# Decode attention beside a gated FFN on one core: head 0 of K loaded in two halves and taken out of VectorE's loop, the three large buffers at multiples of 4096 bytes

## The chip, the core and the metric

The kernel runs on one core of one Trainium2 chip. A core has TensorE (PE in the profile, PEld for its weight loads), VectorE (DVE), ScalarE (ACT), GpSimd (POOL) and SyncE (SP), which each run their own list of instructions and wait for one another through semaphores, and 16 DMA engines that move data between the main memory and the on-chip buffers (SBUF). The metric is the device time of one execution in microseconds, lower is better; times given are medians of several executions.

## What is computed

One token of a decoder layer in fp32. The input row x (576 values) is normalized; an attention block with 32 heads of 128 and a cache of 16384 positions, and a gated FFN of width 4608, both take the normalized row, and both results are added to x:

```
xn = _layernorm(x)
q = (xn @ wq).reshape(B, Sq, H, Dh).transpose(0, 2, 1, 3)
scores = einsum("bhqd,bhkd->bhqk", q, k_cache) * (Dh ** -0.5)
p = softmax(scores)
o = einsum("bhqk,bhkd->bhqd", p, v_cache)
out = x + o.transpose(0, 2, 1, 3).reshape(B, Sq, H * Dh) @ wo \
        + (gelu(xn @ w_gate) * (xn @ w_up)) @ w_down
```

K and V are 32 x 16384 x 128 fp32 each, 8.39 MB a head and cache, 537 MB of the 588 MB that the kernel reads. Each byte is used once.

## The kernel before

**Buffers.** Three large buffers, `slot_a`, `slot_b` and `slot_v` (`sa`, `sb`, `sv` in the code), hold 64 KB in each of the 128 partitions: one head of one cache, partition p holding 128 consecutive positions. They lie one behind the other in SBUF from byte 27904 of a partition on (`SLOT_AT`, L36; the allocation is at L124). Smaller tensors lie below. The weights pass through the same three buffers, before the attention and after it.

**Order.** Nothing is scheduled by a planner: each engine's list is written by hand. Outside the loops the class `Order` (L40) keeps a log of who wrote or read which columns, and puts the waits that follow from it ahead of an operation (`o.op`, behind `dve`, `act`, `pe_op`) or a DMA (`o.dma`, behind `load`). Inside the loops the semaphores are explicit: `take(e, s, n)` (L332) waits for `s` to reach n and takes n off.

**SP's queue.** All large loads are issued by SP, in this order: the q, gate and up weights; K of head 0 into `sb` and of head 1 into `sa` (L349 to L351, `load_k` counting on the semaphores `s_k[0]` and `s_k[1]`); V of head 0 into `sv`; then a loop of 15 passes, two heads each (L354): wait until DVE has released the K buffer (`s_kf`), load K of head h+2, wait until PE has released the V buffer (`s_vf`), load V of head h+1. After the loop come the first 28 row blocks of w_down into `sb`, V of head 31, the other w_down rows and the pieces of wo.

**One head.** ACT copies the head's q, spread over the partitions by PE, into `qs` (L398; `s_qd` tells DVE). DVE multiplies the K buffer in place by `qs` (L382, 128 x 16384), tells ACT through `s_qf` that `qs` may be overwritten, reduces each 128 products to a score in `S` (L384, result 128 x 128; two halves of `S` for even and odd heads), releases the K buffer (`s_kf`), takes each partition's largest score (L387) and, after a transposition by PE, the largest of all, negated (L389). ACT computes the exponentials `pe` and their sum (L402). PE multiplies them with V in 32 steps (L372) into `po` and releases the V buffer. A loop of 16 passes on DVE (L376) handles heads 0 and 1, 2 and 3, and so on, with `sb` for even and `sa` for odd heads.

**Before and after.** Ahead of head 0, DVE finishes the hidden row `hT` of the FFN (L322). Behind the loop it adds up the first 28 blocks of w_down, scaled by `hT` (L414 to L417), and PE projects the attention's result with wo; the last pieces of wo go into columns of `sb` that are already used up.

Of the kernel before, what the change touches and what calls it, by code (L numbers as in the profile page):

```python
# [10 lines left out]
ALU = mybir.AluOpType  # L11
AX = mybir.AxisListType

P = 128
H, SK, DH = 32, 16384, 128
D, DF = 576, 4608
R = SK // P
SUB = 64
# [14 lines left out]
WO_A = 20  # L33
WO_Q = 8
QUART = D // 4
SLOT_AT = 27904  # L36
SLOT_B = R * DH * 4


# [78 lines left out]
@with_exitstack  # L118
def kernel(ctx: ExitStack, tc: tile.TileContext, x, k_cache, v_cache, wq, wo, wg, wu, wd, out):
    nc = tc.nc  # L120
    ends = tc.alloc_semaphore("ends")
    slots = []
    for i, name in enumerate(("slot_a", "slot_b", "slot_v")):
        t = nc.alloc_sbuf_tensor_at(name, [P, R * DH], F32, offset=SLOT_AT + i * SLOT_B)  # L124
        SIZES[t.name] = R * DH
        slots.append(t.ap())
    i = nc.sync.dma_start(slots[0], wq[:DM].rearrange("(p j) f -> p (j f)", j=DJ)).then_inc(ends, 64)
    tc.no_tile_sem_insts.add(i.ins.name)
    tc.add_to_no_dep_group("first", i.ins)
    tc.declare_fence(nc.sync.nop().ins, group="first")  # L130
    with tc.tile_critical(sync_engine=mybir.EngineType.SP):
        decode(tc, x, k_cache, v_cache, wq, wo, wg, wu, wd, out, slots, ends)
    tc.no_sync_barrier()
    nc.sync.wait_ge(ends, 64)
# [19 lines left out]
def decode(tc, x, k_cache, v_cache, wq, wo, wg, wu, wd, out, slots, s_ends):  # L154
    nc = tc.nc
    o = Order(tc)
# [3 lines left out]
    def sem():  # L160
        return tc.alloc_semaphore(f"d{next(names)}")

    def sbuf(name, *shape):
        n = 1
        for s in shape[1:]:
            n *= s
        t = nc.alloc_sbuf_tensor(name, [P, n], F32)
        SIZES[t.name] = n
        return t.ap()[: shape[0]]

    def psum(name, banks):
        t = nc.alloc_psum_tensor(name, [P, 512 * banks], F32)
        SIZES[t.name] = 512 * banks
        return t.ap()

    kv, vv = (c.rearrange("b h (p n) d -> p (b h) (n d)", p=P) for c in (k_cache, v_cache))
# [7 lines left out]
    sa, sb, sv = slots  # L184
# [5 lines left out]
    qcur, qs = sbuf("qcur", 1, DH), sbuf("qs", P, DH)  # L190
    S = sbuf("scores", P, 2 * R)
# [3 lines left out]
    pm, nm, nb = sbuf("pm", P, 1), sbuf("nm", P, 1), sbuf("nb", P, 1)  # L195
    small = sbuf("small", P, 32)
    oT = sbuf("oT", P, WO_T)
    assert nc.sbuf_base <= SLOT_AT, nc.sbuf_base

# [3 lines left out]
    pt, pb, pc = pg[:, 512:1024], pg[:, 1024:], psum("pc", 1)  # L203
# [5 lines left out]
    def dve(name, out, *ins, **kw):  # L209
        o.op("vector", lambda e: getattr(e, name)(out, *ins, **kw), out, *[a for a in ins if isinstance(a, bass.AP)],  # L210
             *[a for a in kw.values() if isinstance(a, bass.AP)])
# [5 lines left out]
    def load(dst, src, **kw):  # L217
        o.dma(dst, src, sem(), **kw)
        return dst
# [13 lines left out]
    for i in range(2):  # L233
# [6 lines left out]
    s_q, s_m, s_n, s_o, s_e, s_v, s_po, s_pq, s_pt, s_pb, s_pc, s_vf, s_kf, s_qf, s_qd, s_d, s_a = (  # L240
        tc.alloc_semaphore(f"h{n}") for n in range(17))
    s_k = [tc.alloc_semaphore(f"k{n}") for n in range(2)]
# [45 lines left out]
    def q_part(h):  # L288
        r, lo = 32 * (h // (H // 4)), h % (H // 4) * DH
        return qb[r : r + 1, lo : lo + DH]  # L290
# [41 lines left out]
    def take(e, s, n=1):  # L332
        e.wait_ge(s, n).then_inc(s, -n)  # L333

    def head(h):
        return bass.ds(h, 1)
# [6 lines left out]
    def load_k(h, dst, s):  # L343
        nc.sync.dma_start(dst, kv[:, head(h), :].rearrange("p h f -> p (h f)")).then_inc(s_k[s], 16)
# [1 line left out]
    def load_v(h):  # L346
        nc.sync.dma_start(sv, vv[:, head(h), :].rearrange("p h f -> p (h f)")).then_inc(s_v, 16)

    for h, dst in ((0, sb), (1, sa)):  # L349
        o.wait("sync", [], [dst])  # L350
        load_k(h, dst, h)  # L351
    o.wait("sync", [], [sv])
    load_v(0)
    with nc.sync.Fori(0, (H - 2) // 2) as i:  # L354
# [18 lines left out]
               for k in range(32)], s_po)  # L373
        nc.tensor.drain().then_inc(s_vf, 1)

    with nc.vector.Fori(0, H // 2):  # L376
        for s, kt in ((0, sb), (1, sa)):
            blk = kt.rearrange("p (n d) -> p n d", d=DH)
            sc = S[:, s * R : s * R + R]
            take(nc.vector, s_k[s], 16)  # L380
            take(nc.vector, s_qd)
            nc.vector.tensor_mul(blk, blk, qs.unsqueeze(1).to_broadcast([P, R, DH])).then_inc(s_d, 1)  # L382
            nc.vector.wait_ge(s_d, 1).then_inc(s_qf, 1)
            nc.vector.tensor_reduce(sc, blk, axis=AX.X, op=ALU.add).then_inc(s_d, 1)  # L384
            nc.vector.wait_ge(s_d, 2).then_inc(s_kf, 1)
            take(nc.vector, s_d, 2)
            nc.vector.reduce_max(pm, sc, axis=AX.X).then_inc(s_m, 1)  # L387
            take(nc.vector, s_pt)
            nc.vector.tensor_reduce(nm[:1], pt[:1, :P], axis=AX.X, op=ALU.max, negate=True).then_inc(s_n, 1)  # L389

    for h0, n in ((0, 6), (6, 8), (14, 8), (22, 8), (30, 2)):
        row, lo = divmod(min(h0 + 2, H - 1), H // 4)
        with nc.scalar.Fori(0, n) as i:
# [11 lines left out]
            src = q_part(min(h0 + 2, H - 1)) if n == 2 else qb[32 * row : 32 * row + 1, bass.ds(i * DH + lo * DH, DH)]  # L405
# [102 lines left out]
```

## Time and profile before

| what | value |
|---|---|
| median of three runs | 1366.23 us (1365.65 to 1366.27) |
| the profiled execution, its own time | 1364.84 us |
| its span, first to last instruction | 1363.0 us |
| DVE busy | 1158.4 us |
| PE busy | 446.3 us |
| read from main memory | 587.60 MB |
| loads of K and V | 64 of 8.39 MB |

A line of the timeline has the start, the duration, the engine, the source line, the operation with its output and input, how many were merged, and in brackets how long the engine had been idle before it and what released it. Several instructions of one kind in a row are merged into one line that begins with the first. "DVEq" or "PEq" as releaser is a semaphore wait of the engine's own sequencer, whatever set the semaphore. A page's rows in 40 slices stand for 34.1 us each. A K buffer that has landed shows in DVE's multiplication, where DVE had been waiting; a V buffer in the first of PE's matmuls into `po`.

### The profile page before, as it was taken

How to read it: one execution, taken by the hardware profiler on the slowest of the kernel's cores; microseconds unless marked ns; L12 is line 12 of the kernel's file. 1: busy time of each engine (PE TensorE's matmuls, PEld its weight loads, DVE VectorE, ACT ScalarE, POOL GpSimd, SP SyncE). 2: the span in 40 equal slices, each digit the busy share in tenths (PEclk: the TensorE clock that was granted, in tenths of full speed). 3: DMA queues.
4: the chain of work that ended last, by engine and by line, in shares of the span. 5: the costliest groups of instructions: out<-in, count | busy, mean ns of one | idle time of the engine just before them, and what ended most of it. 6: DMA issues, size and time to landing. Idle time of an engine off the chain costs nothing. (4 is left out here: it accounts for less than half of the span.)

```text
span 1363.0 us, 7778 instructions
## 1 busy us (share of the span) xinstructions
PE 446.3 (33%) x3012; PEld 161.7 (12%) x3012; DVE 1158.4 (85%) x193; ACT 67.8 (5%) x234; POOL 1.0 (0%) x7
## 2 busy tenths in 40 slices
PE   2431233333322333323222333333223333232236
PEld 1110101111111111101111111011011111011112
DVE  1049999999998888898888888998888888988882
ACT  0000000000000000000000000000000000000000
POOL 0000000000000000000000000000000000000000
PEclk9675666666556666665566666665566666655568
DMA  9999999999999999999999999999999999999998
GB/s 401 446 424 431 431 440 437 431 435 431 435 437 431 433 431 431 446 435 431 431 439 433 433 431 431 446 435 431 431 435 437 433 431 431 444 437 431 430 437 349
DMA packets 11683, 587.69 MB, mean 431 GB/s; under 512 B 1303, under 2 KB 1309, under 8 KB 1694
## 3 DMA queue, kind: packets, MB, share of 16 engines
q1 hardware_dynamic: 11668, 587.60, 99.7%
q8 instruction: 5, 0.08, 0.0%
q10 hardware_dynamic: 10, 0.01, 0.0%
HBM read 587.60 MB, written 0.00 MB: 431 GB/s over the span
## 5 line engine op out<-in xcount | busy, mean ns | idle before, releaser
L329 PE MATMUL po<-slot_v,pe 128*4 128x512 f32 x2048 | 291.7, 733 | 532.6 <-PEq L333 532.6
L382 DVE TENSOR_TENSOR slot_b<-slot_b,qs 128x16384 f32<-128x16384 f32 x16 | 275.6, 17226 | 38.0 <-DVEq L333 38.0
L382 DVE TENSOR_TENSOR slot_a<-slot_a,qs 128x16384 f32<-128x16384 f32 x16 | 275.6, 17226 | 30.6 <-DVEq L333 30.6
L384 DVE TENSOR_REDUCE scores<-slot_a 128x128 f32<-128x16384 f32 x16 | 275.5, 17220 | 2.3
L384 DVE TENSOR_REDUCE scores<-slot_b 128x128 f32<-128x16384 f32 x16 | 275.5, 17220 | 2.3
L329 PEld LDWEIGHTS po<-slot_v,pe 128*4 128x4 f32 x2048 | 56.2, 98 | 740.9 <-issue 740.9
L365 PE MATMUL pg<-ident,pm 128*1 128x128 f32 x32 | 11.9, 371 | 287.3 <-PEq L333 287.3
L329 PE MATMUL pc<-same,z 128*128 128x1 f32 x256 | 59.8, 355 | 0.0
L395 ACT ACTIVATE z<-po 128x512 f32<-128x512 f32 x32 | 19.1, 597 | 783.1 <-ACTq L333 783.1
L329 PEld LDWEIGHTS pc<-same,z 128*128 128x128 f32 x256 | 57.1, 328 | 0.5
L210 DVE TENSOR_TENSOR slot_v<-pg,same 128x396 f32<-128x396 f32 (+1 forms) x6 | 3.3, 558 | 51.9 <-PE pg L207 51.7
L365 PEld LDWEIGHTS pg<-ident,pm 128*1 128x1 f32 x32 | 2.5, 79 | 292.6 <-issue 292.6
L389 DVE TENSOR_REDUCE nm<-pg 1x1 f32<-1x128 f32 x32 | 8.9, 279 | 21.5 <-DVEq L333 21.5
L329 PE MATMUL pg<-nm,ones 1*128 1x1 f32 x64 | 17.7, 343 | 18.5 <-PEq L333 18.5
L329 PE MATMUL pqs<-qcur,ones 1*128 1x128 f32 x64 | 14.8, 312 | 25.3 <-PEq L333 25.3
L210 DVE SCALAR_TENSOR_TENSOR slot_b<-slot_b,hT 128x576 f32<-128x576 f32 x27 | 22.1, 819 | 0.9
L400 ACT ACTIVATE nb<-pg 128x1 f32<-128x1 f32 x32 | 5.5, 171 | 292.3 <-ACTq L333 292.3
L329 PEld LDWEIGHTS pg<-nm,ones 1*128 1x128 f32 x64 | 15.9, 306 | 27.9 <-issue 27.9
L387 DVE TENSOR_REDUCE pm<-scores 128x1 f32<-128x128 f32 x32 | 9.1, 286 | 8.2 <-DVEq L333 8.2
L329 PEld LDWEIGHTS pqs<-qcur,ones 1*128 1x128 f32 x64 | 9.6, 186 | 53.9 <-issue 53.9
L207 PE MATMUL pg<-slot_b,z 128*32 128x396 f32 (+1 forms) x72 | 8.8, 661 | 17.5 <-DMA slot_b<-in_B_w_gate_dram 17.5
L402 ACT ACTIVATE pe<-scores,nb 128x128 f32 x32 | 12.8, 401 | 9.6 <-ACTq L333 9.6
(79 smaller groups left out, 115.3 us busy)
## 6 DMA issues: line engine op xcount, KB each, us to landing
slot_b<-in_B_w_down_dram SPq DMA_DIRECT2D x1, 8064.0 KB, 42.0
slot_b<-in_B_w_gate_dram SPq DMA_DIRECT2D x1, 6912.0 KB, 54.9
slot_a<-in_B_w_up_dram SPq DMA_DIRECT2D x1, 6912.0 KB, 38.2
slot_a<-in_A_wo_dram SPq DMA_DIRECT2D x1, 3456.0 KB, 41.0
slot_v<-in_B_w_gate_dram SPq DMA_DIRECT2D x1, 2304.0 KB, 28.8
slot_v<-in_B_w_up_dram SPq DMA_DIRECT2D x1, 2304.0 KB, 36.8
slot_a<-in_B_w_down_dram SPq DMA_DIRECT2D x1, 2304.0 KB, 28.1
slot_a<-in_A_wo_dram SPq DMA_DIRECT2D x1, 2304.0 KB, 33.2
```

Source lines behind the costliest of these rows:

```text
L207: o.op("tensor", lambda e: e.matmul(outp, lhsT, rhs, start=start, stop=stop), outp, lhsT, rhs, signal=signal)
L210: o.op("vector", lambda e: getattr(e, name)(out, *ins, **kw), out, *[a for a in ins if isinstance(a, bass.AP)], *[a for a in kw.values() i ...
L329: i = nc.tensor.matmul(dst, lhs, rhs, start=start, stop=stop)
L365: nc.tensor.transpose(pt[:1, :P], pm, ident).then_inc(s_pt, 1)
L382: nc.vector.tensor_mul(blk, blk, qs.unsqueeze(1).to_broadcast([P, R, DH])).then_inc(s_d, 1)
L384: nc.vector.tensor_reduce(sc, blk, axis=AX.X, op=ALU.add).then_inc(s_d, 1)
L387: nc.vector.reduce_max(pm, sc, axis=AX.X).then_inc(s_m, 1)
L389: nc.vector.tensor_reduce(nm[:1], pt[:1, :P], axis=AX.X, op=ALU.max, negate=True).then_inc(s_n, 1)
L395: nc.scalar.activation(z, PO, AF.Copy).then_inc(s_o, 1)
L400: nc.scalar.activation(nb, pb[:, :1], AF.Copy, scale=SCALE).then_inc(s_a, 1)
L402: nc.scalar.activation(pe, S[:, bass.ds(i % 2 * R, R)], AF.Exp, bias=nb, scale=SCALE, accum_out=lsum[:, bass.ds(i + h0, 1)]).then_inc(s_e, 1)
```

## The change

Two things are changed. First, K of head 0 is loaded by two DMAs of 128 x 32 KB, and DVE handles the halves one behind the other: multiplication and reduction of the first, then of the second. These go through `load` and `dve`, so their waits come from the log, and they no longer count on `s_k[0]`. DVE releases the K buffer for SP and `qs` for ACT after the second reduction. DVE's loop has 15 passes, an odd head and an even one in each, and head 31 stands behind the loop. Second, the three buffers begin at byte 28672 of a partition (7 x 4096) instead of 27904; with 65536 bytes each, all three then begin at multiples of 4096.

```
-SLOT_AT = 27904
+SLOT_AT = 28672
...
-    for h, dst in ((0, sb), (1, sa)):
-        o.wait("sync", [], [dst])
-        load_k(h, dst, h)
+    parts = [(sb[:, i * SUB * DH : (i + 1) * SUB * DH], S[:, i * SUB : (i + 1) * SUB]) for i in range(R // SUB)]
+    for i, (dst, _) in enumerate(parts):
+        load(dst, kv[:, 0, i * SUB * DH : (i + 1) * SUB * DH])
+    o.wait("sync", [], [sa])
+    load_k(1, sa, 1)
...
-    with nc.vector.Fori(0, H // 2):
-        for s, kt in ((0, sb), (1, sa)):
-            blk = kt.rearrange("p (n d) -> p n d", d=DH)
-            sc = S[:, s * R : s * R + R]
...
+    def highest(sc):
+        nc.vector.reduce_max(pm, sc, axis=AX.X).then_inc(s_m, 1)
+        take(nc.vector, s_pt)
+        nc.vector.tensor_reduce(nm[:1], pt[:1, :P], axis=AX.X, op=ALU.max, negate=True).then_inc(s_n, 1)
+
+    def scores_of(kt, s):
+        sc = S[:, s * R : s * R + R]
+        blk = kt.rearrange("p (n d) -> p n d", d=DH)
+        take(nc.vector, s_k[s], 16)
+        take(nc.vector, s_qd)
+        nc.vector.tensor_mul(blk, blk, qs.unsqueeze(1).to_broadcast([P, R, DH])).then_inc(s_d, 1)
+        nc.vector.wait_ge(s_d, 1).then_inc(s_qf, 1)
+        nc.vector.tensor_reduce(sc, blk, axis=AX.X, op=ALU.add).then_inc(s_d, 1)
+        nc.vector.wait_ge(s_d, 2).then_inc(s_kf, 1)
+        take(nc.vector, s_d, 2)
+        highest(sc)
+
+    take(nc.vector, s_qd)
+    for src, sc in parts:
+        blk = src.rearrange("p (n d) -> p n d", d=DH)
+        dve("tensor_mul", blk, blk, qs.unsqueeze(1).to_broadcast([P, SUB, DH]))
+        dve("tensor_reduce", sc, blk, axis=AX.X, op=ALU.add)
+    nc.vector.wait_ge(o.sem["vector"], o.count["vector"]).then_inc(s_kf, 1)
+    nc.vector.nop().then_inc(s_qf, 1)
+    highest(S[:, :R])
+    with nc.vector.Fori(0, (H - 2) // 2):
+        scores_of(sa, 1)
+        scores_of(sb, 0)
+    scores_of(sa, 1)
```

More of the change, by code (lines that the diff above doesn't have):

```diff
@@ L374, in decode @@
         nc.tensor.drain().then_inc(s_vf, 1)
-    with nc.vector.Fori(0, H // 2):
-        for s, kt in ((0, sb), (1, sa)):
-            blk = kt.rearrange("p (n d) -> p n d", d=DH)
-            sc = S[:, s * R : s * R + R]
[L380 to L389, printed above, removed]
+    def highest(sc):
[25 more added lines that the diff above has]
+    scores_of(sa, 1)
     for h0, n in ((0, 6), (6, 8), (14, 8), (22, 8), (30, 2)):
```

## The prediction

> **What bounds the kernel now.** I read the page first: the span, the busy shares, the DMA rows and the chain that ended last.
>
> ```profile
> span 1363.0 us, 7778 instructions
> PE 446.3 (33%) x3012; PEld 161.7 (12%) x3012; DVE 1158.4 (85%) x193; ACT 67.8 (5%) x234; POOL 1.0 (0%) x7
> DMA  9999999999999999999999999999999999999998
> GB/s 401 446 424 431 431 440 437 431 435 431 435 437 431 433 431 431 446 435 431 431 439 433 433 431 431 446 435 431 431 435 437 433 431 431 444 437 431 430 437 349
> q8 instruction: 5, 0.08, 0.0%
> HBM read 587.60 MB, written 0.00 MB: 431 GB/s over the span
> DMA 6%; DVE 1%; PE 0%; issue 0%; DVEq 0%
> ```
>
> VectorE (DVE) is busy for 85% of the span, but the DMA engines read 9 in every slice and 8 in the last. The kernel reads 587.60 MB at a nearly constant rate. The chain has only its last 7% or so resolved, and most of that is DMA. Next, the busy time by stage (window, length, PE, PEld, DVE, ACT, POOL, clock, DMA share, GB/s), which shows where the rate is below its best:
>
> ```profile
> 4.00:95.06 91.06, 38.61 (x334) 14.33 (x334) 11.45 (x25) 3.11 (x8) 0.00 (x0) 0.82 1.00 430
> 95.06:1274.33 1179.27, 372.54 (x2321) 134.67 (x2321) 1085.25 (x124) 60.02 (x214) 0.00 (x0) 0.61 1.00 434
> 1274.33:1359.18 84.85, 34.71 (x349) 12.55 (x349) 59.38 (x37) 3.39 (x12) 0.00 (x0) 0.69 0.98 422
> ```
>
> From K0's arrival to K31's the rate is 434 GB/s with the engines fully busy. To see whether anything is lost there, I took the timeline of DVE, where each multiplication on a K buffer starts either when DVE is free or when the buffer lands (bracket: idle time before it).
>
> ```profile
> 86.94 0.20 DVE L210 SCALAR_TENSOR_TENSOR hT<-tt,gu 128x36 f32<-128x36 f32 x1
> 95.06 17.23 DVE L382 TENSOR_TENSOR slot_b<-slot_b,qs 128x16384 f32<-128x16384 f32 x1 [7.92 <-DVEq L333]
> 112.43 17.22 DVE L384 TENSOR_REDUCE scores<-slot_b 128x128 f32<-128x16384 f32 x1
> 129.90 0.29 DVE L387 TENSOR_REDUCE pm<-scores 128x1 f32<-128x128 f32 x1 [0.26 <-DVEq L333]
> 131.12 17.23 DVE L382 TENSOR_TENSOR slot_a<-slot_a,qs 128x16384 f32<-128x16384 f32 x1
> 385.67 17.23 DVE L382 TENSOR_TENSOR slot_b<-slot_b,qs 128x16384 f32<-128x16384 f32 x1 [0.68 <-DVEq L333]
> 1235.69 17.23 DVE L382 TENSOR_TENSOR slot_b<-slot_b,qs 128x16384 f32<-128x16384 f32 x1 [2.55 <-DVEq L333]
> 1274.33 17.22 DVE L382 TENSOR_TENSOR slot_a<-slot_a,qs 128x16384 f32<-128x16384 f32 x1 [2.55 <-DVEq L333]
> ```
>
> Late in the loop a head takes 1274.33 - 1235.69 = 38.64 us, of which DVE waits 2.55 for K: DVE needs about 36.09 us a head, the two transfers of a head 38.64, or 19.32 us each (16.78 MB in 38.64 us is 434.2 GB/s). So DMA sets the pace. From K0's landing (95.06, DVE had waited 7.92) to K31's (1274.33) lie 61 loads: K1 to K31 and V0 to V29. 61 x 19.32 = 1178.5; measured 1179.27. **All that the queue loses between those points is 0.8 us.** Where it is lost, the PE's rows on V and SP's issues show:
>
> ```profile
> 133.57 8.47 PE L329 MATMUL po<-slot_v,pe 128*4 128x512 f32 x64
> 172.57 9.44 PE L329 MATMUL po<-slot_v,pe 128*4 128x512 f32 x64 [2.86 <-PEq L333]
> 211.31 8.85 PE L329 MATMUL po<-slot_v,pe 128*4 128x512 f32 x64 [5.00 <-PEq L333]
> 327.61 8.73 PE L329 MATMUL po<-slot_v,pe 128*4 128x512 f32 x64 [12.68 <-PEq L333]
> 366.24 9.88 PE L329 MATMUL po<-slot_v,pe 128*4 128x512 f32 x64 [14.82 <-PEq L333]
> 68.16 0.33 SPq L344 DMA_DIRECT2D slot_b<-in_A_k_cache_dram  x1
> 130.00 0.34 SPq L344 DMA_DIRECT2D slot_b<-in_A_k_cache_dram  x1
> 142.37 0.34 SPq L347 DMA_DIRECT2D slot_v<-in_A_v_cache_dram  x1
> 166.01 0.33 SPq L344 DMA_DIRECT2D slot_a<-in_A_k_cache_dram  x1
> ```
>
> By the pace V0 lands at 95.0 + 38.64 = 133.6 and V1 at 172.3. K2 was issued only at 130.00, 3.6 us before the queue's last load (V0) was through; V1's matmuls start at 172.57. V1 to V5 is 155.04 us, against 4 x 38.64 = 154.56; V5 to V6 is 38.63, on pace. So about 0.3 us goes at K2's late issue and 0.5 us in the next four heads, and nothing after that. My reading is that K2's descriptors reach some DMA engines after these have run dry.
>
> **The change part by part.** (1) *K0 in halves.* K0 is issued as two DMAs of 128 x 32 KB into the same buffer, in the same place of SP's queue. The first half waits only for the gate steps that read it, so its issue moves forward from 68.16 by a few us. The up weights are still in flight then (PE gets them at 75.54), so no byte moves sooner. SP issues one DMA more, 0.33 us long, behind the same cover.
>
> ```profile
> 75.54 7.43 PE L207 MATMUL pg<-slot_a,z 128*32 128x396 f32 x72 [3.73 <-DMA slot_a<-in_B_w_up_dram]
> 1332.00:1350.00 18.00, 16.09 (x144) 5.21 (x136) 4.80 (x8) 0.96 (x3) 0.00 (x0) 0.83 1.00 427
> ```
>
> The cost of shorter rows isn't shown for 32 KB. From below it is 0. From above I take the stretch with wd's and wo's rows, 9 to 28 KB long, at 427 GB/s: K0's 8.39 MB would take 19.65 us against 19.33, +0.3 us. 32 KB is nearer to the 64 KB rows than the shortest of those; I take +0.1, and it is on the path, because every later load queues behind K0.
>
> The Trainium skill, "DMA: Bandwidth & Descriptors", section "Anatomy of one DMA", gives about 2 us fixed to each DMA; an estimate by it is +2.0 us here, which would make the sum a loss of 1.5 us. The trace disagrees for DMAs queued behind one another: at 19.32 us for 8.39 MB, two loads run at 434.2 GB/s with no room for 2 us each.
>
> (2) *DVE starts on the first half.* It lands 9.7 us before K0's 95.0, at about 85.4; DVE is free after hT, at 87.14 (86.94 + 0.20), so it starts at about 87.3 instead of 95.06. Two multiplications and two reductions of half the size take the 34.45 us of one pair (17.23 + 17.22), plus about 0.2 us for two more starts and 0.3 for gaps between dependent instructions (112.43 - 95.06 - 17.23 = 0.14 each). The second half has landed by 95.1, long before DVE reaches it at 104.9. End: 122.3. K0's buffer is free at 122.4 instead of 130.00, **7.6 us earlier**, and K2 is issued 11 us before V0 is through: the dry spell at 133 should go. K1's multiplication starts at about 123.6 (was 131.12), and K3's issue moves from 166.01 to about 158.5. ACT's copy of the next q, which waits for the first multiplication in the loop, now waits for the end of the second reduction; it is then done 0.5 us later, ahead of DVE's next multiplication, which first has the two maxima (1.2 us) to do. V1's issue at 142.37 doesn't move, since V0's landing and PE set it.
>
> From then on DVE is ahead by 7.6 us until it catches up with the transfers; it gains 2.55 us a head, so it meets them near K5 instead of K8 (385.67, the first wait of 0.68 there). None of this is time by itself: it ends as longer waits for K.
>
> (3) *Worth.* At most the 0.8 us above. The 0.3 at the refill I count in full; of the 0.5 after it, half, since I don't know that it stems from the refill. That is -0.55. From below the gain is 0, if some engines run slow for another reason.
>
> (4) *DVE's loop.* 15 passes instead of 16, heads 0 and 31 written out. The waits and operations of a head are the same. Leaving the loop happens between heads 30 and 31, where DVE waits 2.55 us for K31 anyway; should it take longer, K31's buffer is released late. The loads behind it then have V31's 19.3 us ahead of them. A program that is some fifteen instructions longer may need one more piece of code: five pieces are 0.08 MB, so 16 KB each, 0.6 us on one of the 16 engines (434/16 = 27 GB/s). It is on the path only if this engine ends last. I count 0 and keep +0.6.
>
> (5) *Buffers at 28672 instead of 27904.* No instruction changes. The buffers stay 65536 bytes apart, so their place relative to one another is the same, and only the common offset moves, from 6.8 x 4096 to 7 x 4096. The trace has no buffer at a multiple of 4096, so the effect is bounded by rates: even the weight stretch at 427, with other offsets inside the buffers and shorter rows, is within 1.7% of 434, which both ways would be 1179 x 0.017 = 20 us. I take 0: the rate in the cache loads is the same to the third digit for all three buffers, and looks like a fixed limit of the engines.
>
> The same page of the Trainium skill, section "How a descriptor splits into AXI transactions", lets only a start off a 256-byte boundary cost extra; 27904 is 109 x 256, so by it nothing changes. Its section "Where 436 GB/s comes from" has a ceiling of 435.2 GB/s; an estimate by it for the whole 587.60 MB is 3.1 us less than at 434.2, the most that alignment could bring. No run here shows either yet.
>
> Sum: +0.1 - 0.55 = about **-0.5 us**. The profiled execution took 1364.84 us (span 1363.0 and 1.8 around it), so 1364.3 by it. The three timed runs, 1365.65 to 1366.27, lie 0.8 to 1.4 us above it; the same difference from their median of 1366.23 gives **1365.7 us**. If the extra 1.4 us is a larger dry spell at the same place, the gain goes to 2.2; with shorter rows and code at their upper ends and no gain, the loss is 0.9. The tail doesn't move: K31's landing, V31 and the out projection's rows come in the same order behind a full queue.
>
> **The rivals.** *A. No effect on the end.* The 0.8 us isn't due to the late K2, or the split costs as much as it gives. 1366.2 to 1366.6. For it: half of the loss comes after the queue is full again. Against: the lost time begins exactly at the refill. *B. The new offset raises the transfers' rate.* Place: all 61 loads and the weights. It decides over the rest from 0.2% of rate, 434.2 to 435.1: 1363.3; 0.3% would be 1362. For it: the rate in the first 95 us is 430, in the rest 434, so something small is lost per row. Against: 434 in window after window looks like a limit. *C. The new offset lowers the rate*, by collisions of the writes with what DVE and PE read from the same buffers. Place: the 1179 us with all three at work; every 1% costs 11.8 us, and it decides from 0.3% (3.5 us, minus the gain): at 1% 1377.5. Against: DVE takes 17.2 us an instruction and PE about 9 us a head at the present common offset with no trace of disturbed transfers. A slower DVE alone would have to lose the 2.55 us of each head before it counted.
>
> **How the numbers follow.** 0.2%, 2.7 us, is about what a measurement of this kernel can tell from no change. Forecast 60%, A 18%, B 13%, C 9%. Forecast and A both lie within 0.2%: same 78%, faster 13%, slower 9%. Range: 1363.6 to 1367.5, which holds the gain of 2.2, the loss of 0.9 and a little beyond, and leaves out B and C.
>
> **What would show it.** Right: four half instructions on DVE from 87.3, K2's issue at 122.4 and K3's at 158.5, V1's matmuls at 172.3, V5's at 327.0 instead of 327.61, 38.64 us a head later on, DVE's first wait for K near K5. Wrong: a pace other than 38.64 (B or C, by its sign), K1's start later than 123.6 by waits of DVE, V1 still at 172.6 (A), six code pieces instead of five, or a gap at K31 longer than 2.55 us followed by a later end. The forecast is wrong above all if the pace moves, as 0.3% of it outweighs all else.

## The result and the profile after

The changed kernel takes 1363.99 us (median of 22 runs, 1363.77 to 1364.27), the kernel before, run beside it, 1365.87 us (22 runs, 1364.28 to 1367.10). The ratio is 0.9986, 95% interval 0.9980 to 0.9992: a gain of 1.9 us, clear of noise, and below the 0.2% that counted as a change. The runs of the changed kernel lie within 0.5 us of one another, those of the kernel before within 2.8 us. The profiled execution of the changed kernel took 1364.05 us.

The page of the changed kernel, its span, DMA rate by slice and code pieces:

```profile
span 1362.2 us, 7778 instructions
GB/s 403 444 424 433 446 439 431 431 431 433 435 431 431 435 446 437 431 431 431 435 433 431 431 439 445 435 431 431 431 437 431 431 433 441 443 433 431 430 434 347
q8 instruction: 5, 0.08, 0.0%
```

The picture is the old one: DMA bounds the kernel, with five code pieces still. DVE's rows (start, duration, tile, in brackets the idle time before) show head 0 in halves, and K31 behind the loop:

```profile
88.28 0.20 DVE L210 SCALAR_TENSOR_TENSOR hT<-tt,gu 128x36 f32<-128x36 f32 x1
88.47 8.69 DVE L210 TENSOR_TENSOR slot_b<-slot_b,qs 128x8192 f32<-128x8192 f32 x1
97.20 8.69 DVE L210 TENSOR_REDUCE scores<-slot_b 128x64 f32<-128x8192 f32 x1
105.80 8.68 DVE L210 TENSOR_TENSOR slot_b<-slot_b,qs 128x8192 f32<-128x8192 f32 x1
114.52 8.69 DVE L210 TENSOR_REDUCE scores<-slot_b 128x64 f32<-128x8192 f32 x1
124.76 17.23 DVE L388 TENSOR_TENSOR slot_a<-slot_a,qs 128x16384 f32<-128x16384 f32 x1
307.37 17.22 DVE L388 TENSOR_TENSOR slot_b<-slot_b,qs 128x16384 f32<-128x16384 f32 x1 [1.28 <-DVEq L333]
346.06 17.22 DVE L388 TENSOR_TENSOR slot_a<-slot_a,qs 128x16384 f32<-128x16384 f32 x1 [2.61 <-DVEq L333]
423.33 17.22 DVE L388 TENSOR_TENSOR slot_a<-slot_a,qs 128x16384 f32<-128x16384 f32 x1 [2.61 <-DVEq L333]
1273.36 17.23 DVE L388 TENSOR_TENSOR slot_a<-slot_a,qs 128x16384 f32<-128x16384 f32 x1 [2.60 <-DVEq L333]
```

DVE starts as soon as `hT` is ready. The pace of the transfers is unchanged, two heads in 423.33 - 346.06 = 77.27 us, 38.64 a head. K31 lands at 1273.36 instead of 1274.33, so what these two profiles differ by (1364.05 and 1364.84) is gained before that. SP's issues and PE's rows on V show where:

```profile
123.56 0.35 SPq L344 DMA_DIRECT2D slot_b<-in_A_k_cache_dram  x1
143.71 0.34 SPq L347 DMA_DIRECT2D slot_v<-in_A_v_cache_dram  x1
159.64 0.33 SPq L344 DMA_DIRECT2D slot_a<-in_A_k_cache_dram  x1
133.43 9.95 PE L329 MATMUL po<-slot_v,pe 128*4 128x512 f32 x64 [6.23 <-PEq L333]
172.03 9.43 PE L329 MATMUL po<-slot_v,pe 128*4 128x512 f32 x64 [8.68 <-PEq L333]
326.58 8.95 PE L329 MATMUL po<-slot_v,pe 128*4 128x512 f32 x64 [17.99 <-PEq L333]
```

K2 is issued 10 us ahead of V0's landing instead of 3.6. From V0 to V1 it is now 38.60 us (39.00 before), from V1 to V5 154.55 (155.04 before): 4 x 38.64 = 154.56. Nothing is lost any more, neither at K2 nor in the four heads behind it. In the kernel before, PE's row on V0 has no wait in brackets: there PE comes to V0 only when head 0's chain is through, and V0 may have landed a little sooner. The same holds below for every kernel with K2 at 129.8 or later, so the losses read from V0 to V1 are the least that they can be.

### The profile page after: what moved, and what is told of

The parts are those of the page before. It is cut to its first block, busy times and chain, and to the rows that moved or that the text cites. A ratio compares the mean times of both kernels' runs of the same rounds, so it can differ in the third digit from the quotient of the medians.

```text
span 1362.2 us, 7778 instructions
## 1 busy us (share of the span) xinstructions
PE 447.9 (33%) x3012; PEld 162.4 (12%) x3012; DVE 1158.7 (85%) x195; ACT 67.9 (5%) x234; POOL 1.0 (0%) x7
## 5 line engine op out<-in xcount | busy, mean ns | idle before, releaser
L388 DVE TENSOR_TENSOR slot_b<-slot_b,qs 128x16384 f32<-128x16384 f32 x15 | 258.4, 17226 | 31.3 <-DVEq L333 31.3
L390 DVE TENSOR_REDUCE scores<-slot_b 128x128 f32<-128x16384 f32 x15 | 258.3, 17220 | 2.2
L210 DVE TENSOR_REDUCE scores<-slot_b 128x64 f32<-128x8192 f32 x2 | 17.4, 8686 | 0.1
L210 DVE TENSOR_TENSOR slot_b<-slot_b,qs 128x8192 f32<-128x8192 f32 x2 | 17.4, 8686 | 0.0
```

## The experiments

Theory 1 is the prediction's: the gain is K2's earlier issue, which keeps the DMA queue filled. Theory 2 is the new offset of the buffers, theory 3 the new form of the loop. The ratios are to runs of the kernel before on the same chip.

This table gathers what follows. "K2", "V1" and "V5" are the issue of K2 and the first matmul on V1 and V5, "K31" is DVE's start on K31 and "copy" its copy of the finished output, all in us of the profiled execution, whose own time stands ahead of them.

| kernel | median (runs) | profiled | K2 | V1 | V5 | K31 | copy |
|---|---|---|---|---|---|---|---|
| before, 1st profile | 1365.87 (22) | 1364.84 | 130.00 | 172.57 | 327.61 | 1274.33 | 1359.79 |
| before, 2nd | 1365.46 (8) | 1365.06 | 130.06 | 173.06 | 327.93 | 1274.66 | 1360.11 |
| before, 3rd | 1365.44 (8) | 1365.45 | 130.16 | 172.85 | 328.30 | 1275.02 | 1360.49 |
| changed | 1363.99 (22) | 1364.05 | 123.56 | 172.03 | 326.58 | 1273.36 | 1359.01 |
| offset alone | 1365.18 (11) | 1365.18 | 130.16 | 173.32 | 327.92 | 1274.65 | 1360.12 |
| halves alone | 1363.98 (11) | 1363.96 | 122.51 | 172.21 | 326.75 | 1273.54 | 1359.00 |
| one part | 1365.70 (11) | 1366.74 | 129.78 | 173.62 | 328.17 | 1274.89 | 1361.77 |
| 6.5 us added, 1st | 1365.14 (11) | 1364.00 | 128.89 | 172.32 | 326.87 | 1273.65 | 1359.06 |
| 6.5 us added, 2nd | 1365.65 (8) | 1365.38 | 130.15 | 173.39 | 328.23 | 1274.95 | 1360.43 |
| 4.4 us added | 1364.03 (11) | 1364.12 | 128.27 | 172.42 | 326.97 | 1273.76 | 1359.17 |
| 8.7 us added | 1366.26 (11) | 1366.53 | 132.01 | 173.38 | 328.40 | 1275.13 | 1361.57 |
| 17.4 us added | 1374.99 (4) | 1374.32 | 139.89 | 181.26 | 336.23 | 1282.95 | 1369.37 |
| quarters | 1364.30 (11) | 1364.52 | 123.69 | 172.56 | 327.11 | 1273.81 | 1359.32 |

### The offset alone, and the halves alone

The kernel before with one line changed, and the changed kernel with the same line changed back:

```diff
-SLOT_AT = 27904
+SLOT_AT = 28672
```

> The kernel before with the three buffers at 28672, nothing else. Theory 1 (the gain is K2's earlier issue, which keeps the DMA queue filled): time as before, 1365 to 1367; K2 issued near 130.0, V5's matmuls near 327.6 as before. Theory 2 (the gain is the new offset): 1364.0 like the changed kernel, V5's matmuls near 326.6 although K2 is still issued near 130.

> The changed kernel with the buffers back at 27904. Theory 1: 1364.0 as the changed kernel, within 0.3 us, K2 issued near 123.6, V5's matmuls near 326.6. Theory 2: 1365.9 as before.

The offset alone gives a ratio of 0.9996 (0.9987 to 1.0005): no difference that can be told. The halves alone give 0.9987 (0.9978 to 0.9996) and the changed kernel's time. With the offset alone PE's rows still have the loss at K2:

```profile
133.73 8.42 PE L329 MATMUL po<-slot_v,pe 128*4 128x512 f32 x64
173.32 9.10 PE L329 MATMUL po<-slot_v,pe 128*4 128x512 f32 x64 [3.46 <-PEq L333]
```

39.59 us from V0 to V1. Theory 2 falls; the whole gain is in the halves. The Trainium skill, "DMA: Bandwidth & Descriptors", section "How a descriptor splits into AXI transactions", lets a read cost more when it doesn't start at a multiple of 256 bytes. It doesn't speak of where a transfer writes, and both offsets are such multiples, so by it nothing is gained. The times agree: 1363.98 and 1363.99 us at the two offsets.

### Head 0 out of the loop, but in one part

```diff
-SUB = 64
+SUB = 128
```

> The changed kernel with head 0 outside DVE's loop, but K0 in one DMA and handled in one piece, so DVE starts when all of K0 is there. Theory 1: as before, 1365 to 1367, K2 issued near 130. Theory 3 (the gain comes from the new form of the loop and the waits, not from the earlier start): 1364.0 to 1364.5.

The ratio is 0.9998 (0.9989 to 1.0007), K2 is issued at 129.78, and the time is that of the kernel before. The new form of the loop is worth nothing by itself: theory 3 falls. The profiled execution, 1366.74 us, was the second longest of the eleven, and its rows show how much a late K2 can cost:

```profile
129.78 0.34 SPq L344 DMA_DIRECT2D slot_b<-in_A_k_cache_dram  x1
133.53 10.00 PE L329 MATMUL po<-slot_v,pe 128*4 128x512 f32 x64
173.62 8.74 PE L329 MATMUL po<-slot_v,pe 128*4 128x512 f32 x64 [4.06 <-PEq L333]
```

From V0 to V1 it is 40.09 us, 1.45 above the pace, where the first profile of the kernel before had 0.36.

### The lead taken back

Part of the first half's reduction is done a second time, which changes no result and keeps DVE busy before K0 is released:

```diff
         dve("tensor_reduce", sc, blk, axis=AX.X, op=ALU.add)
+        if src is parts[0][0]:
+            dve("tensor_reduce", sc[:, :48], blk[:, :48, :], axis=AX.X, op=ALU.add)
```

> The changed kernel with K0 in two DMAs and DVE starting on the first half, but three quarters of the first half's reduction done a second time, about 6.5 us of DVE, so that the lead is gone: K2 issued at about 130.1 as before. Theory 1: as before, 1365 to 1367, V5's matmuls at 327 to 328. If the split of the DMA, or the order of DVE's work, were the gain in itself: 1364.0.

The eleven runs fell into two groups, five from 1363.93 to 1364.14 and six from 1365.14 to 1366.13. The profiled one is of the first group: K2 at 128.89, V0 to V1 38.61 us, nothing lost. That missed both expectations, and asked for a second profile.

> The kernel with 6.5 us of DVE work added once more, which ended at about 1364.0 in some executions and at 1365.1 to 1366.1 in others. Theory 1a: when hT is ready near 87.0, K2 is issued near 128.9 and nothing is lost (V5's matmuls near 326.9); when it is ready near 88.4, K2 is issued near 130.3 and V5 is at 327.5 or later.

All eight runs of that submission took 1364.98 to 1366.30. The first and the second profile, the end of `hT` and K2's issue:

```profile
87.02 0.20 DVE L210 SCALAR_TENSOR_TENSOR hT<-tt,gu 128x36 f32<-128x36 f32 x1
128.89 0.35 SPq L344 DMA_DIRECT2D slot_b<-in_A_k_cache_dram  x1
```

```profile
88.28 0.20 DVE L210 SCALAR_TENSOR_TENSOR hT<-tt,gu 128x36 f32<-128x36 f32 x1
130.15 0.35 SPq L344 DMA_DIRECT2D slot_b<-in_A_k_cache_dram  x1
133.72 9.69 PE L329 MATMUL po<-slot_v,pe 128*4 128x512 f32 x64
173.39 8.63 PE L329 MATMUL po<-slot_v,pe 128*4 128x512 f32 x64 [3.46 <-PEq L333]
```

The same program, with `hT` 1.26 us later, issues K2 1.26 us later and loses 1.0 us from V0 to V1. So there is an edge between 128.9 and 129.8 (the earliest issue with a loss, in the kernel with one part): K2 has to be issued 3.8 to 4.8 us before PE starts on V0 (133.53 - 129.78 and 133.71 - 128.89). Only one profile stands for each of the two groups of runs; that the others divide by `hT` in the same way isn't shown.

### Less lead, and a late K2

The same edit with 32 columns (4.4 us), with all 64 (8.7 us), and with both halves' reductions done twice (17.4 us):

```diff
+            dve("tensor_reduce", sc[:, :32], blk[:, :32, :], axis=AX.X, op=ALU.add)
```

> The changed kernel with half of the first half's reduction done a second time, about 4.4 us of DVE: K2 issued near 127, 2 us ahead of the profiled run with 6.5 us (128.89, no loss there, but half of its other runs at 1365.1 to 1366.1). Theory 1a (there is a threshold: K2's first data needs about 4.5 us from the issue, and the leading DMA engines are through with V0 at about 132): all runs at 1363.7 to 1364.4. Rival (the loss fades gradually with the lead): median 1364.5 to 1365.

> The changed kernel with the first half's whole reduction done a second time, 8.7 us of DVE: K2 issued near 131.2, 1.2 us later than in the kernel before. Theory 1a with dry time alone as price: 1 us more than before, 1366.5 to 1367.5. Rival (the price is a restart of the engines that ran dry, and hardly the dry time): as before, 1365 to 1366.5, with V1's matmuls at 173.0 to 174.5.

> The changed kernel with both halves' reductions done a second time, 17.4 us of DVE: K2 issued near 140, 10 us later than before. Theory 1a: the queue stands still from about 132 to 133.5 until about 143, so 9.5 to 11 us more than the changed kernel, 1373.5 to 1376, V1's matmuls at 181.5 to 183.5, and the pace of 38.64 us after that. If K2's issue were not the cause: under 1366.

With 4.4 us added, K2 came at 128.27 in the profiled run (`hT` was late there too) and all eleven runs took 1363.77 to 1364.44: the lead can shrink from 10 us to 5.5 at no cost. So the loss doesn't fade in gradually over that stretch. With 8.7 us K2 came at 132.01 and the median is 1366.26, 2.3 us above the changed kernel and 0.5 above the runs of the kernel before beside it (1365.80; ratio 1.0001, 0.9992 to 1.0010): below what dry time alone would have made of it. It lies in the rival's range, as V1 at 173.38 does. With 17.4 us the median is 11.0 us above the changed kernel. The windows of this kernel show the queue standing still (after the engines' busy times, the last two columns are DMA's share and GB/s):

```profile
120.00:130.00 10.00, 0.00 (x0) 0.00 (x0) 9.96 (x2) 0.00 (x0) 0.00 (x0) 0.50 0.97 419
130.00:132.00 2.00, 0.00 (x0) 0.00 (x0) 1.97 (x2) 0.00 (x0) 0.00 (x0) 0.50 0.23 98
132.00:134.00 2.00, 0.00 (x0) 0.00 (x0) 2.00 (x1) 0.00 (x0) 0.00 (x0) 0.50 0.00 0
138.00:140.00 2.00, 0.00 (x0) 0.00 (x0) 1.74 (x2) 0.18 (x1) 0.00 (x0) 0.50 0.00 0
140.00:142.00 2.00, 1.19 (x5) 0.91 (x5) 1.27 (x3) 0.24 (x2) 0.00 (x0) 0.50 1.51 524
142.00:144.00 2.00, 2.00 (x12) 1.55 (x15) 2.00 (x1) 0.79 (x5) 0.00 (x0) 0.50 0.45 197
```

The share of 1.51 shows that the bytes of a row (64 KB, one partition's) are all counted where it begins. So the last rows of V0 begin in 130 to 132, and nothing begins until K2, issued at 139.89, starts all engines: 524 GB/s for 2 us are 16 rows of 64 KB, as many as there are engines. They begin within 2.1 us of the issue, where theory 1a supposed 4.5 us to K2's first data. K2 comes 7.88 us later here than with 8.7 us added, and so does V1 (181.26 - 173.38): with an emptied queue the delay is paid one for one, and V1's matmuls begin 41.37 us after K2's issue in both. Theory 1 holds from both sides.

The same profile in windows of 0.2 us gives a reason for the edge. The last 16 rows of V0 begin between 128.8 and 131.0, and the first 16 of K2 between 140.8 and 141.6, 0.9 to 1.7 us behind the issue. A row takes about 2.4 us, an estimate from 16 rows on each engine in 38.64 us. If the 16 rows are one to an engine, the first engine runs dry near 131.2, and to be sure to reach it by then K2 has to be issued by about 129.5, which lies inside the edge measured.

### More parts

```diff
-SUB = 64
+SUB = 32
```

> The changed kernel with K0 in four parts of 128 x 16 KB. DVE can't start earlier than at 88.3, when the hidden row is done, so K2's issue stays near 123.6 to 124. Theory 1a: 1363.9 to 1364.2, no gain and no loss. If each further DMA cost 2 us on the path: 1368; if more lead were still worth something: below 1363.7.

1364.30 (1364.14 to 1364.52), 0.3 us above the changed kernel, whose runs reach up to 1364.27, and just above the range expected; K2 at 123.69, no more lead, since DVE starts at `hT` either way. If the two further DMAs on the path are what costs it, that is some 0.15 us each; the profile doesn't settle it, as K31 lies only 0.05 to 0.45 us behind the four profiles of kernels with K0 in halves that lose nothing at K2. The Trainium skill, "DMA: Bandwidth & Descriptors", section "Anatomy of one DMA", gives its 2 us for a DMA that GpSimd issues. An estimate by it would be 4 us here. Measured are 0.3, so for DMAs that SP issues and that queue behind one another it doesn't hold.

### The kernel before, two more profiles

> The kernel before, unchanged, for a second profile of it, since the first was one of its fastest executions (1364.84 against a median of 1365.87). Theory 1b (the price of the same dry spell varies from one execution to the next): K2 issued at 129.8 to 130.2 again, but another sum of losses between V0 and V5 and in the tail; V5's matmuls between 327.5 and 329, the end later by the same. Rival (something elsewhere varies): V5 at 327.6 as in the first profile and the rest lost later.

> The same once more, a third sample. Theory 1b: V5's matmuls between 327.5 and 329, not the same as in the other two by some tenths. Rival: 327.6.

V5 is at 327.61, 327.93 and 328.30 in the three profiles, against 326.58 in the changed kernel, and K31 1.0, 1.3 and 1.7 us later than there. K2 was issued within 0.16 us each time. The sum lost differs from one execution to the next, and so does its place: the third profile loses 0.47 us from V0 to V1, little to V2 (38.69), and again at V4 and V5:

```profile
250.31 9.13 PE L329 MATMUL po<-slot_v,pe 128*4 128x512 f32 x64 [7.75 <-PEq L333]
289.28 8.41 PE L329 MATMUL po<-slot_v,pe 128*4 128x512 f32 x64 [10.23 <-PEq L333]
328.30 9.38 PE L329 MATMUL po<-slot_v,pe 128*4 128x512 f32 x64 [13.18 <-PEq L333]
```

38.97 and 39.02 us there, though the queue is filled by then: already K3, at 166.17, is issued 6.7 us ahead of V1's matmuls.

## Why the prediction was right, point by point

**What bounds the kernel** was read rightly: the transfers' pace of 38.64 us a head stands in all kernels, and only what the queue loses can be won.

**The steps of the change.** DVE's four half instructions take 8.69 us each, as expected, but start at 88.47, not 87.3: `hT` was late. The same matmuls on the up weights took 7.43 us in the first profile and 8.90 in this one:

```profile
75.41 8.90 PE L207 MATMUL pg<-slot_a,z 128*32 128x396 f32 x72 [3.92 <-DMA slot_a<-in_B_w_up_dram]
```

So K2's issue is at 123.56 (forecast 122.4) and K3's at 159.64 (158.5); with the halves alone, where `hT` was earlier, K2 is at 122.51. V1's matmuls came at 172.03 (172.3), V5's at 326.58 (327.0). DVE first waits for K at K6 (307.37, 1.28 us), forecast near K5. The split was priced at 0.1 us; the quarters, at 0.3 us for two more DMAs, fit that. The offset was priced at nothing, and is nothing with a late K2 and with an early one. Leaving the loop ahead of K31 costs nothing (the wait for K31 is 2.60 us, 2.55 before).

**The size was wrong, and so was one bound.** The forecast was 0.5 us, measured are 1.9 (1.1 to 2.7 by the interval). The step that failed is (3), "At most the 0.8 us above." It took the loss of one profiled execution as the ceiling, and that execution was among the fastest of the kernel before, 1.0 us under the median of 22. The same step counted only half of the 0.5 us behind the refill: it goes with the refill, as it is gone in each of the five profiles with K2 at 128.9 or sooner (V1 to V5 154.54 to 154.55 us) and stands in six of the eight with a later one (154.84 to 155.45; the offset alone and the one part have 154.60 and 154.55). The sentence that let the gain go to 2.2 us, if the slower runs had a larger dry spell at the same place, came nearest, and it kept the time inside the range. That is in part luck: its condition is shown only in part.

The three profiles of the kernel before account for 1.0 to 1.7 us up to K31. None of them is of one of its slowest runs. The kernel with one part, which behaves as it does, shows a second place: from K31 to the output copy it takes 86.88 us in its profile, against 85.65 in the changed kernel and 85.46 in the kernel before. The two with a late K2 have 86.4. What costs 0.8 to 1.2 us in the tail there stays open.

**The rivals.** A (no effect) is ruled out by the interval. B and C, the offset in either direction, are ruled out by the offset alone: its interval, 0.9987 to 1.0005, leaves out the gain of 0.2% and the loss of 0.3% from which they were to decide.

## What to carry to other kernels

Where transfers set the pace, look for the one place at which the queue runs short, and read it as an edge: here 4.8 us of lead cost nothing, 3.6 us cost 1.9 us in the median. The lead has to cover the variation of whatever sets it as well, here `hT`, which was ready up to 1.6 us sooner or later after one matmul stage. Don't take the loss in one profile as the most that can be won: the spread of the runs, 2.8 us before against 0.5 after, held more of the answer than the profile did.

## What the runs showed of the hardware

Near the edge a late load costs more than the wait for it. With an emptied queue V1's matmuls began 41.37 us after K2's issue. By that count K2 at 130.00 to 130.16 would bring V1 at 171.4 to 171.5, sooner than the 172.0 to 172.6 of the kernels that lose nothing; yet in the kernel before V1 came at 172.57 to 173.06 and, with K2 at 129.78, in the kernel with one part at 173.62. In medians, K2 1.1 us past the last loss-free issue costs 1.9 us, 3.1 us past it 2.3, 11.0 us past it 11.0. In six of the eight profiles with such a loss, some of the next four heads take 0.1 to 0.4 us more than the pace although the queue is filled, in other places in each execution; from V5 on the pace is exact again. That engines which restart at different moments hinder one another is a guess; no run here tells it from other causes.

The same 72 matmuls took 7.43, 8.92 and 8.33 us in the three profiles of the kernel before. Their time goes with the clock granted in the stretch from 75 to 80 us, where they begin: in five of the thirteen profiles it is 0.66, and they take 7.38 to 7.70 us, in the other eight 0.50, and they take 8.15 to 8.94 us. The windows of the kernel before, first profile, and of the changed one (8.90 us):

```profile
75.00:80.00 5.00, 4.46 (x40) 1.55 (x44) 0.00 (x0) 0.00 (x0) 0.00 (x0) 0.66 1.03 446
```

```profile
75.00:80.00 5.00, 4.59 (x32) 1.48 (x36) 0.00 (x0) 0.00 (x0) 0.00 (x0) 0.50 0.99 426
```

In the two profiles with 6.5 us added they took 7.38 and 8.67 us, and that, in a stage which bounds nothing, put K2 on the one side of the edge and on the other.
